# Attention, routed experts and a dense pair of layers on one core: from the routing on, every engine takes its work from one written list

## The chip, the cores and the metric

One core of a Trainium2 chip runs the whole program. It has TensorE (matrix products and, here, all transposes), VectorE, ScalarE, GpSimd and SyncE (SP, which issues most loads). Each engine takes its own instructions in order; between engines they are tied by semaphores. The metric is the device time of one execution in microseconds (us), lower is better.

## The reference

Three steps follow each other on 1536 tokens (2 batches of 768) of width 512 (8 heads of 64).

- Attention: each query sees the keys closer than 16 positions, and beside them 24 summaries, each the maximum of 32 keys (values: the mean), with log 32 added to the score. One softmax over both.
- Routed experts: a token whose product with `w_skip` is not above 0 goes on as it is. Any other token is given to the expert (of 8) with the greatest logit, and becomes `x + gate * (relu(x @ w1[e]) @ w2[e])`, with w1 of 512 x 1024.
- Dense pair: `g(x @ w_in) @ w_out` with 2048 columns between, and `g` 0 below -1, `(h+1)^2/4` up to 1, `h` above. Its weights come as 64-bit floats.

## The kernel before

Attention takes 24 stages of 64 queries by 4 heads' worth of work (`stage_s`, `stage_t`, `stage_pv`: scores, turning of the probabilities, product with the values). When a tile of 128 tokens is complete it is routed: `r1` turns it on TensorE, `r2` multiplies it with the gate (tile `lp`), `r3` takes the maximum and the one-hot on VectorE, `r4` ranks the tokens of an expert by two matmuls with a triangle and with ones (tile `rk`) and works out each token's slot, `r5` scatters the rows by GpSimd to `xf` in device memory. The first 512 rows of `xf` hold tokens that no expert takes; then each expert has a list. `top`, `early` and `late` order the experts by how many tokens they have: position 0 is the largest, known early, positions 1 to 3 are the smallest by what is known after 7 tiles, and positions 4 to 7 the rest. From that order SP reads expert numbers into registers and loads weights.

The first 128 tokens of the largest expert ("first", tiles `fbx`, `hp` of `fb_a`, `yp` of `fb_b`) are gathered early and computed while the last tiles are routed. Then come positions 0 to 7. Each gathers its 32 or 64 rows (one position takes 128 rows more), turns them (`xs`, tile `tpx`), multiplies them by the first layer with the tokens as the stationary side in strips of the array (`as_`, tile `hp`, ScalarE's Relu writes `h`), turns the result (`ts`, tile `tph`), multiplies by the second layer (`bs`, tile `yp`), adds it to the row on VectorE (`ys`) and scatters the row back (`put`). Weights stand in slots of 16 KB a partition named "00" to "13"; a position uses two of them, the first layer and the second, each loaded in two halves (`fetch`, 1.05 MB each). With four pairs of slots position p waits for position p - 4.

The dense pair runs on 3 chunks of 512 tokens. For each of 16 pieces f of the 2048 columns: `mm1` (12 matmuls of 512 columns, tile `hf`), the function `g` on ScalarE and VectorE (`act`), and `mm2` (12 matmuls, tiles `o`). To keep accuracy each operand is split into a rounded half and a rest (`xh`, `xl`, `gh`, `gl`), hence three products. The 64-bit weights are turned into 32-bit ones by three bit operations (`ff_bits`), a rounding on ScalarE and a subtraction on VectorE (`ff_round`), into slots that experts have left. Chunk 0 is the first 512 rows of `xf`, so it needs no expert.

What sets the order: through the attention part every engine follows the order of the code. In the experts' and the dense part only SP and GpSimd do; the order on TensorE, VectorE and ScalarE is drawn from priorities, the place in the code plus the offsets of the table SHIFT. The conversion of the dense weights is a stream of small pieces, of which `fill(n)` places n at a time by the tables FILLS and FFILLS. The four loads of chunk 0's rows stand on SP behind all expert weights (line 857).

Of the kernel before, what the change touches and what calls it, by code (L numbers as in the profile page):

```python
# [42 lines left out]
def tile_net(ctx, tc, q, k, v, w_skip, w_gate, w1, w2, w_in, w_out, out):  # L43
# [12 lines left out]
    xnext = iter(xring * NT)  # L56
# [30 lines left out]
    wg = cp.tile([128, 4, 9], F32, name="wg")  # L87
    placei = cp.tile([1, 18], I32, name="placei")
# [43 lines left out]
    def work_list():  # L132

        def convert(f):
            for step in range(3):
                yield lambda: ff_bits(f, step)
            yield lambda: ff_round(f)

        for f in range(3):
            yield from convert(f)  # L140
            if f:
                for c in (2 * f - 2, 2 * f - 1):
                    yield lambda: st["turn0"](c)
        for f in range(3, NF):
            yield from convert(f)
            if f == YLAST:
                yield lambda: st["ylast"]()

    work = work_list()

    def fill(n):

        for _ in range(n):
            w = next(work, None)
            if w is not None:
                w()

    moves, puts = [], []

    def apart(d, xg, others=()):  # L160

        for o, x in moves:
            if x is not xg and all(x is not y for y in others):
                tc.declare_no_dep(d.ins, o.ins, reason="the blocks have different tokens")
# [13 lines left out]

    @contextmanager
    def shift(name):  # L180
        now = tc.cur_priority
        d = SHIFT.get(name, 0)
        tc.cur_priority = max(0, now + d)
        yield
        tc.cur_priority = now + (tc.cur_priority - max(0, now + d))
# [1110 lines left out]
```

## Time and profile before

| | |
|---|---|
| median of 3 runs | 483.91 us (483.66 to 484.27) |
| the profiled execution | 488.5 us |
| its span, first to last instruction | 486.8 us |
| mean granted clock of TensorE | 0.965 |
| busy: TensorE, VectorE, ScalarE, GpSimd | 455.6, 273.7, 207.9, 70.6 us |
| moved by DMA | 77.19 MB |

A busy TensorE in the profile is one that has a matmul under way, so a busy share near 100% does not say at which clock, or whether the pieces could have come denser; for that the granted clock and the spacing of equal pieces are read. Times in the rows are from the start of the span.

### The profile page before, as it was taken

The numbers are of one execution on the slowest core, as the hardware profiler recorded it, in microseconds if no ns is written. First come the engines' busy times: TensorE is split into PE (matmuls) and PEld (weight loads), VectorE is DVE, ScalarE is ACT, GpSimd is POOL, SyncE is SP. The second block draws the span as 40 slices with busy tenths as digits, with TensorE's granted clock in tenths as the row PEclk, the third lists the DMA queues.
The fourth block names the chain that finished last, engine by engine and source line by source line (L and its number), as shares of the span: only waits on it lengthen the run. The fifth ranks groups of instructions, "written<-read, shape, count | busy, mean of one in ns | idle before, by whom it ended". The sixth has DMA issues, their size and how long they took to land.

```text
span 486.8 us, 8032 instructions
## 1 busy us (share of the span) xinstructions
PE 455.6 (94%) x3010; PEld 332.3 (68%) x3010; DVE 273.7 (56%) x629; ACT 207.9 (43%) x418; POOL 70.6 (15%) x143
## 2 busy tenths in 40 slices
PE   6889999988979995999999999999999999999993
PEld 3567777765434341557778888888888888888882
DVE  3666575785611457599999954433334453333341
ACT  4556555451112122357767765433333443333341
POOL 7001940222330300130000000300000030000003
PEclk9999998995989999699999999999999999999998
DMA  9999999989999999444556600200000020000002
GB/s 196 198 216 194 196 174 230 376 306 374 391 365 398 385 396 380 141 140 140 183 197 224 241 1 25 86 0 1 0 2 0 1 86 0 2 0 1 0 0 94
DMA packets 77104, 77.19 MB, mean 159 GB/s; under 512 B 50606, under 2 KB 58830, under 8 KB 76672
## 3 DMA queue, kind: packets, MB, share of 16 engines
q1 hardware_dynamic: 74176, 68.33, 48.2%
q0 software_dynamic: 2880, 8.25, 4.6%
q8 instruction: 26, 0.43, 0.4%
q14 instruction: 22, 0.18, 0.1%
HBM read 69.44 MB, written 7.76 MB: 159 GB/s over the span
## 4 chain that ended last, share of the span: by engine, by line
issue 42%; PE 29%; DMA 11%; DVE 10%; POOL 5%; SPq 1%; ACT 1%; POOLq 0%; DVEq 0%; ACTq 0%
PE hf L1080 7%; DMA xf<-x,ids 5%; DMA vraw<-in_v_dram 3%; PE s L395 3%; PE o L1121 3%; PE o L1123 2%; PE o L1122 2%; POOL vraw L323 2%; PE hp L229 2%; PE xo L425 2%; POOL out_dram L1133 1%; PE yp L240 1%; PE pt L407 1%; DVE x L914 1%; SPq L303 1%
## 5 line engine op out<-in xcount | busy, mean ns | idle before, releaser
L1080 PE MATMUL hf<-xh,ffw 128*128 128x512 f32 x384 | 126.6, 390 | 0.0
L1080 PEld LDWEIGHTS hf<-xh,ffw 128*128 128x128 f32 x384 | 72.1, 188 | 16.1 <-issue 0.8
L1121 PE MATMUL o<-ffw,g 128*128 128x512 f32 x192 | 76.3, 397 | 0.1
L1122 PE MATMUL o<-ffw,g 128*128 128x512 f32 x192 | 75.5, 393 | 0.0
L1080 PE MATMUL hf<-xl,ffw 128*128 128x512 f32 x192 | 74.9, 390 | 0.0
L1123 PE MATMUL o<-ffw,g 128*128 128x512 f32 x192 | 70.2, 391 | 0.0
L1090 ACT ACTIVATE c<-c,scal 128x512 f32<-128x512 f32 x32 | 23.2, 724 | 74.5 <-DVE c L1089 72.2
L1100 DVE TENSOR_TENSOR hf<-hf,c 128x512 f32<-128x512 f32 x48 | 33.5, 698 | 37.6 <-ACT hf L1098 36.1
L1133 POOL DMA_INDIRECT out_dram<-ob,perm x12 | 11.7, 974 | 247.3 <-DVE ob L1132 162.5
L1106 DVE TENSOR_TENSOR g<-hf,g 128x512 fp32r<-128x512 f32 x48 | 33.1, 690 | 23.4 <-ACT g L1105 23.3
L1089 DVE TENSOR_SCALAR c<-hf 128x512 f32<-128x512 f32 x32 | 22.1, 692 | 40.1 <-PE hf L1080 40.1
L1105 ACT CAST g<-hf 128x512 fp32r<-128x512 f32 x48 | 28.2, 587 | 37.9 <-DVE hf L1100 37.8
L400 ACT ACTIVATE p<-s,nm 128x120 f32<-128x120 f32 x96 | 26.7, 361 | 37.1 <-DVE nm L397 19.8
L1121 PEld LDWEIGHTS o<-ffw,g 128*128 128x128 f32 x192 | 36.1, 188 | 8.8 <-ACT g L1105 1.2
L1123 PEld LDWEIGHTS o<-ffw,g 128*128 128x128 f32 x192 | 36.0, 188 | 8.6 <-DVE g L1106 0.3
L1080 PEld LDWEIGHTS hf<-xl,ffw 128*128 128x128 f32 x192 | 36.1, 188 | 7.5
L1122 PEld LDWEIGHTS o<-ffw,g 128*128 128x128 f32 x192 | 36.1, 188 | 7.0
L914 DVE SCALAR_TENSOR_TENSOR x<-yp,x 32x512 f32<-32x512 f32 (+1 forms) x28 | 20.8, 744 | 10.5 <-PE yp L906 9.6
L395 PE MATMUL s<-pb 64*64 64x120 f32 x384 | 25.7, 275 | 0.0
L397 DVE TENSOR_REDUCE nm<-s 128x4 f32<-128x480 f32 x24 | 15.7, 653 | 15.4 <-PE s L395 12.4
L395 PEld LDWEIGHTS s<-pb 64*64 64x64 f32 x384 | 20.1, 136 | 5.4 <-issue 5.4
L1045 ACT CAST ffw<-cv 128x1024 fp32r<-128x1024 f32 x16 | 16.6, 1046 | 13.3 <-DVE cv L1030 11.4
(221 smaller groups left out, 643.4 us busy)
## 6 DMA issues: line engine op xcount, KB each, us to landing
w<-in_moe_w_dram SPq DMA_DIRECT2D x32, 1024.0 KB, 15.3
raw<-in_moe_w_in_dram SPq DMA_DIRECT2D x16, 512.0 KB, 4.2
raw<-in_moe_w_out_dram SPq DMA_DIRECT2D x16, 512.0 KB
x<-xf SPq DMA_DIRECT2D x12, 264.0 KB, 5.2
raw<-in_k_dram SPq DMA_DIRECT2D x16, 192.0 KB
raw<-in_q_dram SPq DMA_DIRECT2D x16, 192.0 KB, 5.0
vraw<-in_v_dram SPq DMA_DIRECT2D x4, 768.0 KB, 7.8
vw<-in_v_dram SPq DMA_DIRECT2D x13, 192.0 KB, 6.2
```

What stands on the lines that cost most here:

```text
L395: nc.tensor.matmul(s[a, u], tq[a, j], tk[a, j], start=False, stop=u == 3)
L400: nc.scalar.activation(out=p[:, u], in_=s[:, u], func=AF.Exp, bias=nm[:, u:u + 1], scale=1.0)
L914: nc.vector.scalar_tensor_tensor(out=xg[0:n, 0:512], in0=yp[a], scalar=xg[0:n, 512:513], in1=xg[0:n, 0:512], op0=ALU.mult, op1=ALU.add)
L1080: nc.tensor.matmul(hp, w[:, 128 * kk:128 * kk + 128], a[:, kk], start=(n == 0), stop=(n == 11))
L1089: nc.vector.tensor_scalar(out=c, in0=hp, scalar1=-1.0, scalar2=1.0, op0=ALU.max, op1=ALU.min)
L1090: nc.scalar.activation(out=c, in_=c, func=AF.Square, bias=half, scale=0.5)
L1100: nc.vector.tensor_tensor(out=hp, in0=hp, in1=c, op=ALU.add)
L1105: nc.scalar.copy(out=gh, in_=hp)
L1106: nc.vector.tensor_tensor(out=gl, in0=hp, in1=gh.bitcast(F32), op=ALU.subtract)
L1121: nc.tensor.matmul(ops[ch][t], gh[:, a], hi, start=(f == 0), stop=False)
L1122: nc.tensor.matmul(ops[ch][t], gh[:, a], lo, start=False, stop=False)
L1123: nc.tensor.matmul(ops[ch][t], gl[:, a], hi, start=False, stop=(f == NF - 1))
```

## The change

From the end of attention on all engines follow the order of the code. The experts and the first eight pieces of the dense chunk 0 are cut into pieces with one letter each, and one string, ORDER, lists them: X, A, T, B are TensorE's four steps of an expert position, x, a, t, y those of ScalarE and VectorE behind them; U, P, Q, O the same steps of the 128 rows more; R, r, l turn and split chunk 0's rows; M and N are a block of `mm1` and of `mm2`, with c, S, g, G the function between; i, j, k, H, L convert dense weights; F loads a half of a layer of an expert (F40: position 4, half 0), W a piece of dense weights, E gathers rows. After the string, `rest` goes on with piece 8 in fixed steps.

Routing on VectorE is written as generators; `step()` issues one instruction or two of the routing between two instructions of attention, `settle()` the rest. The gather of the block "first" and the loads of position 1 are issued one stage earlier. Position 5 has the 128 rows more (it was 4). Slots: positions 4 and 5 use those of 1 and 2, position 6 those of 3, position 7 those of 5, and the dense weights 0 to 3 those of position 0. The tile of the block "first" stands in another pool (it stood in slot "13"). Chunk 0's 512 rows come in one load into one tile, issued behind the last scatter, with a small one for their token numbers.

```diff
-BIG = (4,)
-ROOM = (64, 32, 32, 32, 160, 32, 64, 32)
+BIG = (5,)
+ROOM = (64, 32, 32, 32, 32, 160, 64, 32)
 LISTS = 1536
 EOFF = 28 * CAP + 8 * LISTS
-SLOTS = (("00", "01"), ("02", "03"), ("10", "11"), ("13", "12"))
-FFSLOTS = ("00", "01", "02", "03", "10", "11", "12", "13")
-NRAW = 4
-FILLS = ((0, 0, 0), (0, 0, 0), (0, 0, 0), (0, 0, 2), (2, 2, 2, 2), (2, 1, 1), (1, 1, 2))
-LAST = 2
-FFILLS = ((2, 1, 2), (2, 0, 2))
-SHIFT = {'bits': 6, 'round': -57, 'act': -1, 'add': -97, 'g': 8, 'y': 18, 'x': -8, 't': 6, 'turn': 0}
-YLAST = 4
-PLACES = {4: 0, 5: 2, 6: 1, 7: 3}
+SLOTS = (("00", "01"), ("02", "03"), ("10", "11"), ("13", "12"), ("02", "03"), ("10", "11"), ("13", "12"), ("10", "11"))
+FFSLOTS = ("00", "01", "02", "03", "13", "12", "10", "11")
+XORDER = (0, 1, 2, 3, 4, 5, 6, 0, 1, 2, 5, 3, 4) + (6, 0, 1, 2, 3, 5, 4, 6, 0) + (1, 2, 3, 4, 5, 6, 0, 1)
+AHEAD = 8
+ORDER = '''
+Z0 i0 j0 k0 X0 x0 A0 X1 a0 x1 T0 H0 A1 t0 L0 B0 F40 a1 i1 F41 j1 k1 W2 H1 R0 y0 F32 R1 F33 r0 R2 r1 l0 r2 l1 R3
+l2 X2 r3 L1 T1 x2 A2 t1 l3 B1 F50 a2 F51 i2 X3 F42 y1 T2 F43 x3 A3 t2 B2 a3 j2 k2 T3 E6 F52 X4 F53 t3 M0 W3 x4
+y2 H2 F60 B3 c0 L2 F61 A4 E7 y3 M1 a4 W4 S0 g0 c1 G0 X5 T4 N0 x5 S1 t4 g1 G1 B4 A5 y4 U0 a5 T5 u0 X6 t5 i3 P0 x6
+j3 k3 W6 H3 B5 F62 F63 p0 L3 P1 y5 A6 p1 i4 j4 k4 W5 H4 Q0 F70 M2 F71 a6 L4 q0 i6 j6 Q1 c2 T6 k6 N1 q1 S2 H6 O0
+t6 L6 g2 G2 i5 j5 k5 H5 M3 F72 o0 F73 L5 W7 B6 c3 S3 X7 y6 g3 M4 x7 G3 A7 c4 i7 M5 j7 a7 S4 k7 g4 N2 c5 G4 i8 j8
+T7 H7 M6 S5 k8 t7 H8 L7 B7 c6 L8 i9 N3 y7 N4 g5 G5 S6 j9 M7 g6 k9 H9 G6 i10 N5 c7 L9 j10 k10 S7 i11 N6 g7 G7 j11
+'''
+PLACES = {4: 2, 5: 0, 6: 1, 7: 3}
...
-            tag = "w" + SLOTS[p % 4][c // 2]
+            tag = "w" + SLOTS[p][c // 2]
...
+        xt, flow = {}, []
+
+        def step():
+
+            while flow:
+                g = flow.pop(0)
+                if next(g, flow) is not flow:
+                    flow.append(g)
+                    return
+
+        def settle():
+            while flow:
+                step()
...
             mx = sm("mx", [128, nt])
             nc.vector.tensor_reduce(out=mx, in_=lt[:, :, 0:8], axis=AX.X, op=ALU.max)
+            yield
             d = sm("d", [128, nt, 8])
             nc.vector.tensor_tensor(out=d, in0=lt[:, :, 0:8], in1=bc(mx), op=ALU.subtract)
             cm = comp[:, ts[0]:ts[0] + nt]
             nc.vector.tensor_scalar(out=cm, in0=lt[:, :, 8], scalar1=0.0, scalar2=None, op0=ALU.is_gt)
+            yield
             val = sm("val", [128, nt, 8])
             nc.vector.scalar_tensor_tensor(out=val, in0=d, scalar=0.0, in1=bce(idx8), op0=ALU.is_lt, op1=ALU.add)
+            nsk = sm("nsk", [128, nt])
...
-            t = wp.tile([128, 12, 128], F32, tag="w13", name="fbx")
-            fb["x"], fb["hT"] = t[:, 0:4], t[:, 4:12]
+            t = b8.tile([128, 16, 128], F32, tag="b8", name="fbx")
+            fb["x"], fb["hT"] = t[:, 0:4], (t[:, 0:4], t[:, 12:16])
+            h = t[:, 4:12].rearrange("p c f -> p (c f)")
...
-        for i in range(3, 2 * NT):
-            if i + 1 < 2 * NT:
-                stage_t(i + 1)
+        for i in range(3, 2 * NT - 1):
+            stage_t(i + 1)
             for _ in range(2 if 5 < i < 8 else 1):
                 if rest:
                     prep(*rest.pop(0))
             if i + 3 < 2 * NT:
                 stage_s(i + 3)
+                step()
             if rest:
                 prep(*rest.pop(0))
-            stage_pv(i)
+            if i == 21:
+                stage_pv(i)
+            for f in pre[i]:
+                f()
+            flow += [f() for f in flows[i]]
+            step()
+            if i != 21:
+                stage_pv(i)
             run_todo(i)
+            step()
+            if i > 15 and i != 18:
+                settle()
+            for f in post.get(i, ()):
+                f()
         for c in range(4):
             fetch(2, c)
-        for f in range(2, NRAW):
-            ff_fetch(f)
-        t, = end = groups[NT - 1]
-        r1(t)
-        r4(of[t - 1])
-        r5(of[t - 1])
+        end, two = groups[NT - 1], groups[NT - 2]
+        fb_x()
+        flow.append(r3(two))
+        step()
+        stage_pv(2 * NT - 1)
+        settle()
+        fb_a(0, (0,))
+        r1(end[0])
+        r4p(two)
+        fb_a(0, (1,))
+        flow.append(r4(two))
+        settle()
         r2(end, 0)
-        fb_x()
-        r3(end)
-        fb_a(0, (0, 1))
-        r4(end)
-        r5(end)
-        late()
         fb_a(0, (2, 3))
-        fb_a(1, range(4))
-        fb_t(0), fb_t(1)
+        flow.append(r3(end))
+        settle()
+        r4p(end)
+        count_p(NT)
+        fb_a(1, (0, 1))
+        fb_a(1, (2, 3))
+        fb_t(0)
+        flow += [r4(end), late()]
+        settle()
+        late_blocks()
+        fetch(3, 0)
+        fetch(3, 1)
+        get_rows()
+        fb_t(1)
         for p in range(NEARLY):
             get(p)
-        fb_b()
+        fb_b(0)
+        fb_b(1)
+        fb_y()
         late_regs()
-        for c in range(4):
-            fetch(3, c)
+        get(4)
         get(BIG[0])
         get((BIG[0], 1))
         st["beyond"] = beyond
 
 
 
-    reads = []
-
...
+    def get_rows():
+
+        t = st["rows"] = b8.tile([128, 4, 512], F32, tag="b8", name="rows")
+        v = xf[0:EARLY].rearrange("(t p) c -> p t c", p=128)
+        for out, c in ((t.bitcast(I32), slice(0, 512)), (perm[:, 0:4].unsqueeze(2), slice(513, 514))):
+            d = nc.sync.dma_start(out=out, in_=v[:, :, c])
+            apart(d, t)
+
+    def get_perm(c, xg):
         nc.vector.tensor_copy(out=perm[:, c:c + 1], in_=xg[:, 513:514].bitcast(I32))
-        return xg
...
+        do = dict(X=X, x=x, A=A, a=a, T=T, t=t, B=B, y=y, U=U, u=u, P=P, p=p_, Q=Q, q=q_, O=O, o=o, Z=Z, R=R, r=r, l=l,
+                  M=M, c=c, S=S, g=g, G=G, N=lambda f: dense.mm2(0, f), H=high, L=low, W=ff_fetch, E=get,
+                  i=lambda f: bits(f, (0,)), j=lambda f: bits(f, (1,)), k=lambda f: bits(f, (2,)),
+                  F=lambda n: fetch(n // 10, n % 10))
+        for word in ORDER.split():
+            do[word[0]](int(word[1:]))
+        dense.rest(AHEAD)
...
+        def step(i, ch, f, n):
             hp = mm1(ch, f)
-
-            act(ch, f, hp, FFILLS[min(i, len(FFILLS) - 1)])
+            c = act(ch, f, hp)
+            runs(n - 1, high)
+            add(hp, c)
+            runs(n, lambda f: bits(f, (2,)))
+            gh(ch, f, hp)
+            gl(ch, f, hp)
+            runs(n - 1, low)
+            runs(n + 1, lambda f: bits(f, (0, 1)))
             if ch + 1 < NC:
...
-        with tc.manual_schedule(engines={EngineType.SP, EngineType.Pool}):
+        with tc.manual_schedule():
             experts(mctx)
-            feed()
     xpool.close()
```

The order on TensorE at the end of the routing, before (`lp` is the last tile's gate product, line 219 the turning of the block "first", `hp_2130` its products, `rk` and `cnt` the last tile's ranks and the counts):

```order
L454 MATMUL lp<-wg,xs 64x9 x8
L219 MATMUL tpx_2108<-ident,x_74 128x128 x4
L229 MATMUL hp_2130<-w_1335,fbx 128x512 x2
L497 LDWEIGHTS tri
L497 MATMUL rk<-ohb,tri 128x8
L498 LDWEIGHTS ones
L498 MATMUL rk<-runs,ones 128x8
L559 LDWEIGHTS ones
L559 MATMUL cnt<-runs,ones 128x8
L229 MATMUL hp_2130<-w_1335,fbx 128x512 x2
```

and of the change, from the first product of the block "first" to the last tile's gate product (`tpx<-ident,x_74` turns the last tile, `rk` are the ranks of the two tiles before it):

```order
L202 MATMUL hp_2057<-w_1336,fbx 128x512
L432 MATMUL tpx<-ident,x_74 128x128 x4
L493 LDWEIGHTS tri
L493 MATMUL rk<-ohb,tri 128x8
L494 LDWEIGHTS ones
L494 MATMUL rk<-runs,ones 128x8
L493 LDWEIGHTS tri
L493 MATMUL rk<-ohb,tri 128x8
L494 LDWEIGHTS ones
L494 MATMUL rk<-runs,ones 128x8
L202 MATMUL hp_2057<-w_1336,fbx 128x512
L443 MATMUL lp<-wg,xs 64x9 x8
```

The turning of "first" and its first product have come ahead of the last tile's turning, and of its first four products, which stood two before and two behind the last tile's ranks, one stands before each matmul step of the routing and two behind `lp`, all ahead of the last ranks.

The order on TensorE from position 2 to 4, before (`yp` second layers, `hp` first layers, `tph` and `tpx` turns; w_2047 and w_2290 are second layers of positions 2 and 3, w_2287 and w_2360 first layers of 3 and 4):

```order
L219 MATMUL tpx<-ident,x_74 128x128 x4
L906 MATMUL yp<-w_2047,hT 32x512 x8
L888 MATMUL hp<-w_2287,xT 32x256 x16
L896 MATMUL tph<-ident,h 128x128 x2
L877 MATMUL tpx<-ident,x_75 128x32 x4
L906 MATMUL yp<-w_2290,hT 32x512 x8
L888 MATMUL hp<-w_2360,xT 32x256 x8
```

and of the change (w_2206 is the first layer of position 3, w_2017 the second of position 2); `hf` is the first dense block:

```order
L1002 MATMUL hp<-w_2206,xT 32x256 x16
L1024 MATMUL yp<-w_2017,hT 32x512 x8
L1012 MATMUL tph<-ident,h 128x128 x2
L990 MATMUL tpx<-ident,x_73 128x32 x4
L1195 MATMUL hf<-xh,ffw 128x512
L1195 MATMUL hf<-xl,ffw 128x512
```

Dense matmuls, which stood behind all experts, now begin behind the second layer of position 2.

SP's queue, before, behind the loads of position 2 (`raw` are dense weights; line 648 reads the late positions' numbers, and position 3's loads follow it):

```order
L1012 DMA raw_2050<-in_moe_w_in_dram 128x4x256
L1014 DMA raw_2050<-in_moe_w_out_dram 128x1024
L1012 DMA raw_2053<-in_moe_w_in_dram 128x4x256
L1014 DMA raw_2053<-in_moe_w_out_dram 128x1024
L648 TENSOR_LOAD placei
```

and of the change, from the second half of position 3's first layer (w_2206) on (`rows` and `perm` are chunk 0's; line 707 reads the late positions' numbers, and position 4's loads follow it):

```order
L136 ISA
L136 DMA w_2206<-in_moe_w_dram 128x2x1024
L961 DMA rows<-xf 128x4x512
L961 DMA perm<-xf 128x4x1
L707 TENSOR_LOAD placei
```

Position 3's first layer and chunk 0's rows stand ahead of the numbers now, and dense weights 2 and 3 behind.

## Rows read from the trace of the kernel before

**Rows 1.** Stretches: length, busy time (x instructions) per engine, granted clock, DMA share, GB/s.
```profile
104.00:136.60 32.60, 26.69 (x152) 14.68 (x147) 20.63 (x128) 6.91 (x17) 11.48 (x12) 0.79 1.02 376
136.60:186.00 49.40, 47.56 (x342) 19.91 (x344) 18.58 (x30) 10.13 (x24) 7.77 (x9) 0.97 1.04 392
186.00:212.30 26.30, 20.58 (x127) 9.00 (x123) 17.80 (x26) 6.81 (x12) 3.94 (x3) 0.81 0.53 190
212.30:252.70 40.40, 40.26 (x176) 32.09 (x173) 38.83 (x46) 29.86 (x45) 3.66 (x2) 1.00 0.55 186
252.70:480.00 227.30, 226.71 (x1010) 186.38 (x1008) 110.08 (x158) 98.29 (x159) 10.20 (x11) 1.00 0.11 40
```

**Rows 2.** Timeline of TensorE, end of routing: start, length, instructions, [idle before, releaser].
```profile
103.43 0.69 PE L425 MATMUL xo<-vw,pts 120*64 120x66 f32 x16
105.71 0.17 PE L497 MATMUL rk<-ohb,tri 128*128 128x8 bf16 x1 [1.59 <-DVE ohb L483]
...
116.38 3.78 PE L229 MATMUL hp<-w,fbx 128*128 128x512 f32 x4 [0.72 <-issue]
119.95 0.21 PE L497 MATMUL rk<-ohb,tri 128*128 128x8 bf16 x1
...
136.64 0.79 PE L877 MATMUL tpx<-ident,x 64*128 64x64 f32 x8 [2.30 <-DMA x<-xf,re]
```

**Rows 3.** The same timeline: an expert's pieces at full rate.
```profile
125.89 0.60 PE L235 MATMUL tph<-ident,fbh 128*128 128x128 f32 x4
...
127.23 7.12 PE L240 MATMUL yp<-w,fbx 128*128 128x512 f32 x16
...
146.22 3.65 PE L906 MATMUL yp<-w,hT 128*64 128x512 f32 x16
149.80 0.44 PE L896 MATMUL tph<-ident,h 128*128 128x128 f32 x2
150.17 1.93 PE L888 MATMUL hp<-w,xT 128*32 128x256 f32 x32
```

**Rows 4.** The same timeline: after the wait for token rows.
```profile
194.96 1.94 PE L219 MATMUL tps<-ident,x 128*128 128x128 f32 x8 [5.52 <-DMA x<-xf]
...
198.08 3.64 PE L906 MATMUL yp<-w,hT 128*32 128x512 f32 x16
```

**Rows 5.** Timeline in the dense part: two blocks' last matmuls, and the last of all.
```profile
457.13 0.39 PE L1080 MATMUL hf<-xh,ffw 128*128 128x512 f32 x1
...
462.60 0.39 PE L1080 MATMUL hf<-xh,ffw 128*128 128x512 f32 x1
...
479.02 0.39 PE L1123 MATMUL o<-ffw,g 128*128 128x512 f32 x1
```

**Rows 6.** Stretch of the dense matmuls alone: those of hf, then of o.
```profile
209.00:252.90 43.90, 24.04 (x96) 18.05 (x97) 9.40 (x14) 13.85 (x23) 1.00 0.51 172
...
209.00:252.90 43.90, 20.45 (x80) 14.71 (x80) 0.00 (x0) 0.00 (x0) 1.00 0.51 172
```

**Rows 7.** Timeline of VectorE, first instruction behind the last rank matmul.
```profile
120.23 0.17 DVE L500 TENSOR_TENSOR sl<-rk,ohb 128x8 f32<-128x8 f32 x1 [3.03 <-PE cnt L559]
```

**Rows 8.** Timeline of GpSimd: first block's gather, last scatter, first expert's gather.
```profile
103.89 1.06 POOL L168 DMA_INDIRECT x<-xf,r  x1 [3.18 <-DVE den L428]
...
122.31 0.97 POOL L173 DMA_INDIRECT xf<-x,si  x1 [4.25 <-DVE nall L563]
129.42 1.23 POOL L168 DMA_INDIRECT x<-xf,re  x1 [6.14 <-DMA xf<-x,si]
```

**Rows 9.** Stretches of 10 us, columns as in rows 1 with GpSimd.
```profile
110.00:120.00 10.00, 8.19 (x52) 4.68 (x50) 5.46 (x38) 1.39 (x4) 2.91 (x3) 0.50 0.99 366
...
150.00:160.00 10.00, 9.42 (x114) 4.27 (x112) 4.06 (x7) 2.62 (x7) 1.90 (x2) 1.00 1.04 397
...
190.00:200.00 10.00, 4.85 (x26) 3.08 (x30) 4.22 (x8) 3.75 (x7) 1.72 (x1) 0.65 0.63 221
```

**Rows 10.** Timeline of SP's queue: loads of expert weights from the fourth expert on.
```profile
134.56 45.65 SPq L129 DMA_DIRECT2D w<-in_moe_w_dram  x20
```

More of the change, by code (lines that the diff above doesn't have):

```diff
@@ L130, in fetch, with apart @@
                           .rearrange("p e k f -> p (e k) f"))
[L132 to L156, printed above, removed]
     moves, puts = [], []
-    def apart(d, xg, others=()):
+    def apart(d, xg):
         for o, x in moves:
-            if x is not xg and all(x is not y for y in others):
+            if x is not xg:
                 tc.declare_no_dep(d.ins, o.ins, reason="the blocks have different tokens")
@@ new lines, in y, with U, u @@
+        def y(p):
+            xg, n, yp = st["x", p], st["n", p], bag.pop(("B", p))
+            for a in sides(n):
+                nc.vector.scalar_tensor_tensor(out=xg[0:n, 0:512], in0=yp[a], scalar=xg[0:n, 512:513],
+                                               in1=xg[0:n, 0:512], op0=ALU.mult, op1=ALU.add)
+            put(p)
+        def U(_):
+            bag["U"] = turned(st["x", more], tile4(128, "tpx"))
+        def u(_):
+            bag["u"] = side("xTm")
+            nc.scalar.copy(out=bag["u"], in_=bag.pop("U"))
@@ new lines, in Q, with q_, O @@
+        def Q(f):
+            tp = bag["Q", f] = tile4(128, "tph")
+            for c in range(4):
+                nc.tensor.transpose(tp[:, c], bag["p"][:, 4 * f + c], ident)
+        def q_(f):
+            if f == 0:
+                bag["q"] = wk.tile([128, 8, 128], F32, tag="hT", name="hTm", bufs=3)
+            nc.scalar.copy(out=bag["q"][:, 4 * f:4 * f + 4], in_=bag.pop(("Q", f)))
+        def O(_):
+            yp = bag["O"] = ps.tile([128, 512], F32, tag="y", name="yp")
+            for kk in range(8):
+                nc.tensor.matmul(yp, bag["q"][:, kk], wx[big, 1][:, kk], start=kk == 0, stop=kk == 7)
@@ new lines, in o, with R, Z @@
+        def o(_):
+            xg = st["x", more]
+            nc.vector.scalar_tensor_tensor(out=xg[:, 0:512], in0=bag.pop("O"), scalar=xg[:, 512:513], in1=xg[:, 0:512],
+                                           op0=ALU.mult, op1=ALU.add)
+            put(more)
+        def R(c):
+            bag["R", c] = turned(st["rows"][:, c], tile4(128, "tps"))
+            if c == 3:
+                st.pop("rows")
+        def Z(_):
+            xTs[0] = tuple(b8.tile([128, 4, 512], F32R, tag="b8", name=n) for n in ("xh", "xl"))
@@ new lines, in r, with l, M, c @@
+        def r(c):
+            nc.scalar.copy(out=xTs[0][0][:, :, 128 * c:128 * c + 128], in_=bag["R", c])
+        def l(c):
+            xh, xl = (z[:, :, 128 * c:128 * c + 128] for z in xTs[0])
+            nc.vector.tensor_tensor(out=xl, in0=bag.pop(("R", c)), in1=xh.bitcast(F32), op=ALU.subtract)
+        dense = feed()
+        def M(f):
+            st["late"] = "h"
+            bag["M", f] = dense.mm1(0, f)
+        def c(f):
+            bag["c", f] = dense.act(0, f, bag["M", f])
+        def S(f):
+            dense.add(bag["M", f], bag.pop(("c", f)))
@@ L1015, in ff_fetch, with bits @@
         raw64[f] = t
[L1017 to L1022 removed]
+    def bits(f, steps=range(3)):
+        for step in steps:
+            if step == 0:
+                odd = f % 2 and f > 6
+                cv[f] = st["wk"].tile([128, 2, 512], I32, tag="h" if odd else "cv", name="cv", bufs=2 if odd else 1)
+            t, o = raw64[f], cv[f]
             if step == 0:
```

468 lines of the change are left out of this document (239 added, 229 removed).

## The prediction

> **What bounds the kernel now.** I read five views, in this order. First the stretches [rows 1]: from 252.7 us TensorE is busy 226.7 of 227.3 us at full clock, from 212.3 to 252.7 it is as full and VectorE is at 38.8 of 40.4 us, so the dense layers are bound by TensorE's matmuls. From 104 to 212.3 us it is not: some 6 us are empty in the first and the third of the three stretches, and the granted clock is 0.79 and 0.81 there. That is where the change works. Then TensorE's rows at the end of the routing [rows 2]: a wait of 1.59 us for VectorE's one-hot, four matmuls at half rate (3.78 us) ahead of the last rank matmul at 119.95, and 2.30 us of waiting for the first gathered tokens, which start to be turned at 136.64. Third, what an expert's pieces cost at full rate [rows 3], and the same piece after TensorE had stood still 5.52 us for token rows [rows 4]: 3.64 us in place of 1.92. Fourth the dense blocks: a pair of blocks, 24 matmuls, repeats every 462.60 - 457.13 = 5.47 us, 0.228 us a matmul, and the last ends at 479.4 [rows 5]. Fifth, how far the dense part is at one moment: by 252.9 us there are 96 + 80 = 176 matmuls done [rows 6], so 180 (eight first-layer blocks M0 to M7, seven second-layer blocks N0 to N6) at 252.9 + 4 x 0.228 = 253.8. From there TensorE needs 479.4 - 253.8 = 225.6 us more.
>
> After the change the same 180 matmuls are the ones that the list holds, among the experts' pieces; what follows is the same 41 + 40 blocks. So the forecast is one number: how much earlier than 253.8 the list's last dense block ends.
>
> **Part by part.** *Routing steps among attention's.* The last rank matmul stands at 119.95. In the new order TensorE has between the end of attention's last-but-two value product (104.1 in [rows 2]) and that matmul: two score matmuls and the last of three (3 x 0.6), the turning of the probabilities, of the last tokens (twice) and of the first block (4 x 0.6), two value products (2 x 0.7), four of the first block's matmuls (a run of eight takes 7.12 [rows 3], so 4 x 0.9) and the ranks (0.6): 9.8 us, plus about 0.7 us of copies between them: 114.6. The wait of 1.59 goes, since the one-hot's steps are issued one stage earlier, and so does the half-rate surplus (3.78 x 1/2) if the clock holds. The first block is turned before the last value product now: its gather, issued at 103.89 [rows 8], must have landed by 108. Its row numbers are worked out one stage (2.9 us) earlier, so I count no wait; its cost, if it landed as late as the later gather's 7.2 us after today's issue, is 3 us. VectorE reaches its first routing instruction behind the rank at 120.23 today after idling 3.03 us for it [rows 7], and the last scatter is issued at 122.31, 2.1 us on; now some 20 instructions of two chains stand there instead of 12, which I take as 0.7 us more. The scatter then goes out at 114.6 + 0.3 + 2.8 = 117.7, 4.6 us earlier [rows 8]. From it to the first turned tokens are 136.64 - 122.31 = 14.3 us, a scatter's landing and a gather's, and both remain.
>
> *The load of the first 512 rows* (1.05 MB) now waits on SP for the same scatter and so moves with the gather; at 397 GB/s [rows 9] that is 2.6 us of all queues. Bounds for the gather: 0, when the queues share and its few bytes come first, and 2.6 + 5.3 us when it stands behind that load and the two loads of the fourth expert (2 x 1.05 MB) that SP now issues before it. I take 1 us, near the lower end, since the gather of today landed in 7.2 us while [rows 1] show 376 GB/s of other traffic, so it did not wait for a queue to drain. The Trainium skill, page DMA: Bandwidth & Descriptors, section Queues, rings and completion order, says that a DMA engine takes turns between the queues that have work, a packet at a time; by it the sum would be as here, by first come first served it would be the second rival below; no row here shows two queues' turns apart. First turned tokens: 136.6 - 4.6 + 1 = 133.0, a gain of 3.6.
>
> *The list.* From there to the 180th matmul takes 253.8 - 136.6 = 117.2 us today. TensorE's own work in that stretch, at full rate: 15 dense blocks x 2.735 = 41.0; first layers of the experts, two of 64 rows at 3.65 and six of 32 at 1.93, 18.9; second layers the same again, 18.9; the extra 128 rows of the large expert, twice 7.12 as the first block's, 14.2; and the turns, 14 small ones at 0.44 and nine at 0.6, 11.6 [rows 3, 5]. Sum 104.6, and the surplus of today is 12.6: 5.5 idle [rows 4], the rest half-rate stretches (0.65 in 190 to 200 [rows 9], worth 3.5 us) and small waits. In the list the rows wait goes, since the 512 rows are turned right after the first expert, some 60 us before the other experts end. What is late next: copies that nothing covers (first tokens' copy 0.7, first activations 0.4, the four row turns behind three PSUM buffers 1.3, some eight of 0.2 to 0.5 later), 4 us; the wait before the first tokens, which grows: the first block ends at 114.6 + 13 = 128, so TensorE stands still some 5 us instead of 2.30, and by the stall of 5.52 us, behind which the pieces are at half rate until 201.7, 6.7 us on [rows 4], I take 8 us at half rate, which cost 4. Bounds for this surplus of mine: 3 (only copies) to 16 (each piece also waits once for its weights). I take 8, so the list gives 12.6 - 8 = 4.6.
>
> *Weights.* A half of an expert's layer is 1.05 MB, 2.6 us at 397 GB/s [rows 9]. The places changed: expert 5 waits for expert 2's, expert 8 for expert 6's. The fifth expert's loads stand on SP behind the second expert's first layer (133.0 + 8 = 141), where SP today starts 20 loads at 134.56 [rows 10]; queues run dry for up to 10 us before it. From 141 on, 22 loads come at 2.6 us in the list's order; the second layer of the fifth expert lands at 167 and is wanted at 171, the seventh's first layer 181 against 186, the last expert's first layer 200 against 214. Its second layer waits for the large expert (203), lands at 211, and is wanted at 225; the dense chunk behind it on SP lands at 213, when VectorE reaches it. So I cost waiting for weights at nothing, with slack of 4 to 14 us; where SP, waiting at its head, is 5 us later than this, the cover is gone.
>
> *Strict order in the dense part.* Today the last matmuls of a block are drawn behind three of the next; now a block's third matmul needs its lower half at once. VectorE needs 38.83/40.4 of its time today [rows 1]; per pair of blocks the new order has the same six instructions. Between 0 and +3 us for the six pairs with conversions left; I take 0.
>
> **Sum.** 3.6 + 4.6 = 8.2 us off the profiled execution, 488.5 (span 486.8) to 480.3. The runs without the profiler have a median of 483.91, 4.6 below; the same difference gives 475.7.
>
> **Rivals.** *All waits covered, clock kept*: the surplus is 3 and the gather costs nothing: 4.6 + 9.6 = 14.2 us, 469.7. For it: only 104.6 us of work in 117; against it: the empty stretch before the first tokens.
> *Gathers behind the loads*: the first tokens come 7.9 us after my 132.0, at 139.9; the list then leaves 4.6 - 3.3 = 1.3: 482.6. Half of that delay gives 478.7. For it: scatter and gather took 14.3 us with the queues full; against it: 7.2 us was enough for the gather.
> *Slower, through the clock*: the place is TensorE from the first tokens on. After 1.6 us of waiting at 104 us the granted clock was 0.50 for 110 to 120 [rows 2, 9], and a stall of 5.5 us brought 0.65. Every microsecond at half rate costs 0.5. If the wait of 5 us and the copies' gaps keep the clock at 1.2 GHz for 16 us beyond my 8, the 8.2 are gone; for 25 us the result is 483.9 - 8.2 + 12.5 = 488.2. It decides from 16 us on. The Trainium skill, page TensorE: Matmul & The Clock Gate, section HAM oscillation — how this bites in real kernels, tells of matmuls that start slow after each wait for a DMA; by that rule every such wait of the list would be paid twice, and the trace agrees at 194.96. Against it: M and N blocks, dense and long, stand between the experts from the fourth on, and in the dense part of today the clock is 1.00 throughout [rows 1].
> *The list is not followed in time*: engines wait for each other as long as before, within 1 us of today, 484.
>
> **Chances.** Forecast 0.55 (471 to 479), all covered 0.13, gathers late 0.17, no change 0.04, slower 0.11. The range 467 to 482 takes in the first three but leaves out the far ends. A change of 0.2%, 1 us, is about what this kernel's runs can tell. Faster 0.85, same 0.04, slower 0.11.
>
> **What would show it.** Last rank matmul near 115 and last scatter near 118; first tokens turned at 132 to 134; the 5.5 us wait for rows gone; granted clock above 0.9 from 140 to 235; the 180th dense matmul near 245.6; no wait of TensorE for a weight over 1 us; 225 to 226 us from there to the last matmul. I am wrong if the first tokens stay near 136.6, if the clock stays at half past 150, or if TensorE waits for weights.

## The result, and the profile after

The changed kernel takes 477.32 us, the median of 4 runs (476.84 to 477.85), beside 484.09 us (483.66 to 484.82) for the kernel before: ratio 0.9859, with a 95% interval of 0.9842 to 0.9876. Measured again beside other runs later, the ratio was 0.9837 (0.9807 to 0.9868). It is faster by 1.4 to 1.6%, some 7 to 8 us. The forecast was 475.7, in a range of 467.0 to 482.0. Its profiled execution took 477.85 us.

First the stretches of [rows 1], here of the changed kernel (columns as there).

```profile
104.00:136.60 32.60, 24.76 (x131) 12.42 (x127) 14.16 (x98) 4.56 (x11) 10.72 (x11) 0.86 0.99 373
136.60:186.00 49.40, 47.64 (x378) 23.82 (x376) 34.10 (x46) 19.77 (x39) 9.86 (x9) 0.99 0.91 336
186.00:212.30 26.30, 26.27 (x109) 14.85 (x106) 19.91 (x25) 11.98 (x19) 3.28 (x3) 1.00 1.00 364
212.30:252.70 40.40, 39.39 (x204) 29.97 (x203) 31.46 (x38) 23.54 (x37) 1.33 (x2) 1.00 0.47 162
252.70:480.00 227.30, 214.40 (x952) 175.18 (x951) 99.72 (x146) 90.24 (x145) 11.69 (x12) 0.99 0.09 34
```

The third line is where the time came from: TensorE busy 26.27 of 26.30 us at full clock, where it was 20.58 at 0.81. VectorE is at 34.10 of 49.40 us in the second line (19.91 before) and at 31.46 of 40.40 in the fourth (38.83 before): its conversions now lie beside the experts. In the first line TensorE is busy for less time than before (24.76 against 26.69 us), at a higher mean clock (0.86 against 0.79): about as much of the stretch is still lost to waiting and half rate.

TensorE's timeline at the end of the routing shows where; it answers to [rows 2].

```profile
104.59 0.64 PE L443 MATMUL lp<-wg,xs 128*64 128x9 f32 x16 [0.16 <-ACT xs L433]
108.79 1.11 PE L192 MATMUL tpx<-ident,x 128*128 128x128 f32 x4 [3.56 <-DMA x<-xf,r]
...
110.92 2.08 PE L202 MATMUL hp<-w,fbx 128*128 128x512 f32 x2
...
117.13 0.17 PE L493 MATMUL rk<-ohb,tri 128*128 128x8 bf16 x1
...
132.60 0.43 PE L990 MATMUL tpx<-ident,x 64*128 64x64 f32 x4 [2.87 <-DMA x<-xf,re]
133.61 5.35 PE L1002 MATMUL hp<-w,xT 128*64 128x512 f32 x16 [0.58 <-ACT xT L994]
```

The waits for one-hots near the end are gone, but TensorE now stands 3.56 us for the first block's gathered tokens, and the last value product, the last tokens and the last ranks stand behind that wait in its order. Behind it the matmuls run at half rate, 2.08 us for two; and behind the second wait, 2.87 us for the first expert's tokens, its first layer takes 5.35 us where it takes 3.65 at full rate. GpSimd's timeline, which answers to [rows 8]:

```profile
101.34 1.06 POOL L149 DMA_INDIRECT x<-xf,r  x1 [6.32 <-PE pt L381]
...
119.53 0.97 POOL L154 DMA_INDIRECT xf<-x,si  x1 [1.70 <-DVE ve L186]
126.47 1.09 POOL L149 DMA_INDIRECT x<-xf,re  x1 [5.97 <-DMA xf<-x,si]
```

The first gather is issued at 101.34, only 2.5 us earlier than before, while TensorE wants it some 9 us earlier: at 105.2, against 114.55 in the kernel before, whose row is

```profile
114.55 1.12 PE L219 MATMUL tpx<-ident,x 128*128 128x128 f32 x4
```

The last two lines of GpSimd's timeline put the end of the routing at 119.53 and the first expert's gather at 126.47; its tokens are turned at 132.60, 6.1 us later.

In the dense part, the end of the list (the last matmul of N6, and M8's first), the two waits of TensorE behind it and the start of the last matmul:

```profile
240.45 0.39 PE L1238 MATMUL o<-ffw,g 128*128 128x512 f32 x1
240.68 0.39 PE L1195 MATMUL hf<-xh,ffw 128*128 128x512 f32 x1
...
272.41 0.66 PE L1177 MATMUL tpf<-ident,x 128*128 128x128 f32 x4 [1.04 <-DVE xl L1185]
...
464.21 0.50 PE L1236 MATMUL o<-ffw,g 128*128 128x512 f32 x1 [0.75 <-ACT g L1219]
...
468.50 0.40 PE L1238 MATMUL o<-ffw,g 128*128 128x512 f32 x1
```

So the path divides like this: first turned tokens 136.64 to 132.60, 4.0 us gained; from there to the end of the list 117.2 to 108.1 us, 9.1 gained; from the end of the list to the start of the last matmul 225.2 us (479.02 - 253.8, [rows 5, 6]) to 227.8, 2.6 lost. That is 10.5 us between these two profiled executions, more than the 6.8 us between the medians: the profiled execution of the kernel before lay above its runs (488.5 beside 484.1).

### The profile page after: what moved, and what is told of

Its sections match the earlier page's. It is cut to its first block, busy times and chain, and to the rows that moved or that the text cites. A ratio compares the mean times of both kernels' runs of the same rounds, so it can differ in the third digit from the quotient of the medians.

```text
span 476.1 us, 8008 instructions
## 1 busy us (share of the span) xinstructions
PE 446.3 (94%) x3010; PEld 327.1 (69%) x3010; DVE 266.1 (56%) x625; ACT 208.8 (44%) x418; POOL 70.0 (15%) x143
## 4 chain that ended last, share of the span: by engine, by line
PE 38%; issue 37%; DMA 8%; DVE 6%; SPq 5%; ACT 2%; POOL 2%; POOLq 0%; DVEq 0%; ACTq 0%
PE hf L1195 6%; PE s L369 4%; SPq L277 3%; PE hp L1002 3%; DMA raw<-in_moe_w_out_dram 3%; PE o L1236 3%; PE o L1237 3%; PE o L1238 2%; PE xo L411 2%; PE yp L1024 2%; PE pt L381 2%; DVE x L1029 2%; DMA vw<-in_v_dram 2%; POOL out_dram L1248 2%; DMA x<-xf,r 2%
## 5 line engine op out<-in xcount | busy, mean ns | idle before, releaser
L1236 PE MATMUL o<-ffw,g 128*128 128x512 f32 x192 | 76.3, 398 | 0.7 <-ACT g L1219 0.7
L1237 PE MATMUL o<-ffw,g 128*128 128x512 f32 x192 | 75.5, 393 | 0.0
L1238 PE MATMUL o<-ffw,g 128*128 128x512 f32 x192 | 75.0, 391 | 0.0
L1204 ACT ACTIVATE hf<-hf,scal 128x512 f32<-128x512 f32 x32 | 21.2, 662 | 85.1 <-DVE c L1203 85.1
L1157 DVE TENSOR_TENSOR ffw<-cv,ffw 128x1024 fp32r<-128x1024 f32 x16 | 19.5, 1219 | 12.8 <-ACT ffw L1152 12.8
```

What stands on the lines that cost most here:

```text
L1204: nc.scalar.activation(out=hp, in_=hp, func=AF.Relu, bias=mone, scale=1.0)
L1236: nc.tensor.matmul(ops[ch][t], gh[:, a], hi, start=(f == 0), stop=False)
L1237: nc.tensor.matmul(ops[ch][t], gh[:, a], lo, start=False, stop=False)
L1238: nc.tensor.matmul(ops[ch][t], gl[:, a], hi, start=False, stop=(f == NF - 1))
```

## The experiments

All times are medians; each ratio is to the kernel before, run on the same chip in the same session. That kernel took 484.1, 487.4, 488.0, 484.9 and 484.6 us in the five sessions, so ratios are compared, not microseconds. The four later sessions ran on different chips; what is the session's and what is the chip's is not told apart here. The control e0 ran beside e5, e7 and e11; e1, e2, e4 and e6 share a session, e8, e9 and e12 another, and e14 has its own.

| run | us | ratio, 95% interval |
|---|---|---|
| changed kernel, first measurement | 477.3 | 0.9859 (0.9842 to 0.9876) |
| e0_control, the same again | 479.6 | 0.9837 (0.9807 to 0.9868) |
| e2_dense_behind | 514.1 | 1.0560 (1.0515 to 1.0605) |
| e5_experts_first | 505.4 | 1.0354 (1.0328 to 1.0381) |
| e9_rows_late | 499.5 | 1.0299 (1.0276 to 1.0323) |
| e6_no_interleave | 480.1 | 0.9845 (0.9810 to 0.9880) |
| e4_value_first | 480.8 | 0.9862 (0.9833 to 0.9891) |
| e11_value_then_first | 480.3 | 0.9855 (0.9822 to 0.9888) |
| e7_turn_first | 477.7 | 0.9785 (0.9756 to 0.9813) |
| e8_busy_before_tokens | 474.1 | 0.9792 (0.9758 to 0.9826) |
| e12_busy_twice | 472.5 | 0.9738 (0.9717 to 0.9758) |
| e14_value_first_busy | 473.4 | 0.9773 (0.9748 to 0.9799) |

**e0_control** was expected at a ratio of 0.984 to 0.988, with a wait of 0.5 to 3.6 us for the first block's gather and 105 to 110 us from the first turned tokens to the 180th dense matmul. The ratio was 0.9837, the wait 4.02 us, both just outside, and the stretch 108.3 us:

```profile
134.10 0.43 PE L990 MATMUL tpx<-ident,x 64*128 64x64 f32 x4 [2.76 <-DMA x<-xf,re]
...
242.43 0.39 PE L1195 MATMUL hf<-xh,ffw 128*128 128x512 f32 x1
...
470.25 0.40 PE L1238 MATMUL o<-ffw,g 128*128 128x512 f32 x1
```

**e1_before_again**: the kernel before, a second profile.

> The kernel before, unchanged, for a second profile. Theory A: the 4.6 us by which its profiled execution (488.5) lies above the runs without a profiler (484.1) belong to that one execution, in the stretch between the first turned tokens (136.64) and the 180th dense matmul (253.8), 117.2 us there: the second profile shows about 484 and 112 to 114 us in that stretch, with the first tokens near 136.6 again. Rival B: the profiler always costs this kernel 4.6 us: the second profile shows 488 and 117 us again.

It took 486.6 us in a session whose median was 487.4. TensorE's timeline of this second profile of the kernel before:

```profile
134.16 0.43 PE L877 MATMUL tpx<-ident,x 64*128 64x64 f32 x4 [1.11 <-DVE ids L207]
...
194.13 1.94 PE L219 MATMUL tps<-ident,x 128*128 128x128 f32 x8 [8.24 <-DMA x<-xf]
...
251.75 1.09 PE L1123 MATMUL o<-ffw,g 128*128 128x512 f32 x4
...
477.45 0.39 PE L1123 MATMUL o<-ffw,g 128*128 128x512 f32 x1
```

Neither theory holds. The profiled execution is not above the runs beside it, so the profiler costs nothing that shows. The 4.6 us are then most likely a difference between executions or sessions; in which session the first profile was taken, the record doesn't say. And the stretch to the 180th dense matmul is long again: 180 have begun by 252.2, 118.0 us behind the first tokens. Two more things are to be seen. The first tokens come at 134.16, 2.5 us before those of [rows 2], with the same code: where the routing ends differs by that much from one execution to the next. And TensorE gained little by it: it waits 8.24 us instead of 5.52 for the token rows, which come at 194.13 against 194.96. In the kernel before, most of what came earlier at the routing's end was given back at the rows: 0.8 of the 2.5 us is left there. Set against e0, this profile divides the gain otherwise than the first pair: 0.1 us at the first tokens (134.16 to 134.10), 9.7 in the list (118.0 to 108.3), 2.6 lost behind it (225.2 to 227.8). That is 7.2 us, near the 6.8 of the runs, and nearly all of it is the list's.

**e2_dense_behind and e5_experts_first**: the dense layers' pieces taken out from among the experts.

```
 e2: ORDER = (all pieces but M c S g G N, in their order) + (M c S g G N, in their order)
 e5: as e2, and i j k H L of chunks 4 and up, W6, W7 also moved behind the last expert
```

> The changed kernel with the 47 pieces of the dense layers' arithmetic (M, c, S, g, G, N) moved in the list behind the last expert, in their own order; the conversions and the loads stay where they are. Theory A: the dense blocks among the experts cover the loads of expert weights. From 140 us some 18 half layers and 6 dense chunks of 1.05 MB have to land, 24 x 2.6 = 63 us, so the last expert cannot be done before about 205; the 15 dense blocks, 41 us, then stand behind it, and the 180th dense matmul comes near 250 in place of 240.7: about 487 us (483 to 491), with waits of TensorE for weights that sum to about 10 us. Rival B: what the list gives comes from the early token rows and the clock that is kept, and the place of the dense blocks is indifferent: 476.5 to 478.5 us.

> The changed kernel with its list sorted: the experts' pieces first, with the early turning of the 512 rows, the conversions of the dense chunks 0 to 3 and the loads of chunks up to 5 where they stand; behind the last expert all arithmetic of the dense layers and the conversions from chunk 4 on, in their own order. Theory A: among the experts the dense blocks cover loads. 22 loads of 1.05 MB from about 140 us on take 57 us, so the last expert's second layer cannot start before 197 to 200, and M0 to N6 with their conversions take 44 us behind that, as they did before (209.6 to 253.8): the 180th dense matmul at 244 to 247 and 4 to 7 us more than the unaltered changed kernel, with TensorE's waits for weights before 200. Rival B: the early rows are the whole gain, experts and dense part could as well stand apart: within 1 us of the unaltered one, with the 180th dense matmul near 241.

Both cost far more than theory A said, in the direction that it said. The waits of TensorE of 140 to 270 us, first e2, then e5:

```profile
PE yp L1024 <- ACT hT L1016: 12.0, 1, 12.0
PE o L1236 <- ACT g L1219: 10.3, 1, 10.3
PE yp L1024 <- DMA w<-in_moe_w_dram: 5.3, 3, 4.2
```

```profile
PE hf L1195 <- ACT ffw L1152: 9.3, 1, 9.3
PE yp L1024 <- DMA w<-in_moe_w_dram: 5.6, 4, 4.1
```

Weights are waited for directly (5.3 and 5.6 us), in e2 half of the 10 us expected. The long waits are of another kind. In e2 ScalarE's copy for the last expert stands in the list behind the rounding of a chunk whose load lands at 213.6, and so TensorE stands 12.0 us for an expert whose weights SP had issued at 199.04, ahead of that chunk. An engine that follows a list passes one late load on to everything behind it. In e5 the conversions came too late instead: VectorE is at 6.61 of 26.30 us from 186 to 212.3 and the chunk is then missing at 244.9. So without the dense blocks among the experts this list loses more than its whole gain; how much of the 26 to 35 us is loads, and how much these two lists' own faults, the runs don't separate. Nor does a run give the kernel before the early load of the 512 rows alone, so whether that needed the written order stays open.

**e9_rows_late**: the one load of 512 rows put behind weights on SP.

```
-        get_rows()                    # ahead of the expert loads
+ ORDER: ... F42 y1 T2 F43 Y0 ... F53 t3 R0 r0 R1 l0 r1 R2 l1 r2 R3 l2 r3 l3 M0 ...   (Y0 = get_rows)
```

> The unaltered changed kernel but for the load of the first 512 rows, which stands on SP behind the loads of the second layer of the fifth expert and not ahead of all of them, and their turning and splitting right before the first dense block M0. Theory A: a load that SP issues behind the weights lands behind them, as the rows did before: SP paces these loads at 2.6 us each from 144.6 on, so the rows are issued near 158 and land 5 to 13 us later; TensorE waits at M0 (158) for 6 to 14 us, and half rate follows: 8 to 16 us over the unaltered changed kernel, 488 to 496 us, ratio 1.000 to 1.017. Rival B: the queues share, a row load is served beside the weights: a wait of at most 3 us, 480 to 484 us, ratio under 0.993.

Theory A holds, and more: SP's issue of the rows, TensorE's wait, and the load's time from issue to landing.

```profile
155.75 4.34 SPq L960 DMA_DIRECT2D rows<-xf  x1
```

```profile
173.39 1.94 PE L192 MATMUL tps<-ident,rows 128*128 128x128 f32 x8 [18.77 <-DMA rows<-xf]
```

```profile
DMA to landing us min/median/max: 17.5/17.5/17.5
```

A load of 1.05 MB that SP issues behind eight half layers and a dense chunk lands 17.5 us later, and TensorE waits 18.77 us where at most 14 were expected; the kernel takes some 22 us more than the control (0.0462 of 485). The gather that GpSimd issued among the same traffic, at 159.48, landed in 6.3 us (381 GB/s from 155 to 172). Both agree with what the Trainium skill, page DMA: Bandwidth & Descriptors, section Queues, rings and completion order, states: a DMA engine takes turns between queues, but consumes one queue's descriptors in order.

**e6_no_interleave**: each routing chain run to its end at once.

```
                 if next(g, flow) is not flow:
                     flow.append(g)
-                    return
```

> The changed kernel with each routing chain run to its end where its next step would stand, instead of one step at a time among attention's instructions. Theory A: single steps hide the latency of a chain; run in one piece, the normalising of attention's values waits behind them on VectorE and TensorE's waits for one-hots come back, as before (1.59 and 0.73 us): the first tokens come about 2 us later, 479.5 us (478.5 to 481). Rival B: VectorE has room enough, the order of its steps is worth nothing: 476.6 to 478 us.

Rival B has the better of it: 0.9845 (0.9810 to 0.9880) against 0.9837 of e0, another session. The waits for one-hots did not come back; TensorE waits 2.08 us at 97.87 instead, and the first tokens come at 133.76, within the spread of the other profiles. Weaving single routing steps among attention's is worth nothing that can be measured here; the interval leaves room for 1.7 us either way.

**e4_value_first and e11_value_then_first**: attention's last value product ahead of the first block.

```
-        fb_x()
         flow.append(r3(two)); step(); stage_pv(2 * NT - 1); settle()
-        fb_a(0, (0,))
         r1(end[0])
+        fb_x(); fb_a(0, (0,))         # e11; in e4 both stand behind r4p(two) and r2(end, 0)
```

> The changed kernel with the turning of the first block's tokens moved behind attention's last value product, the last tokens' turn and the last logits; all of the first block's first-layer matmuls but one stand behind the last rank matmul. Theory A: TensorE's 3.56 us of waiting for the first block's gather holds back the routing's end behind it; now the wait stands behind what the last ranks need, so the last rank matmul comes at 111 to 113 (117.1 in the changed kernel), the last scatter at 114 to 116 (119.5), the first tokens are turned at 128 to 130 (132.6), when the first block ends: about 474 us (472.5 to 475.5). Rival B: from the last scatter to the first turned tokens the queues full of weights decide, or the weights do later: first tokens stay near 132.6, or a wait for weights takes their gain, 476.5 to 478 us.

> The changed kernel with attention's last value product and the last tokens' turn ahead of the first block's turned tokens; otherwise the order of the routing's end is kept, with the first block's matmuls between the steps of the rank chain. Theory A: the wait for the first block's gather holds back only what stands behind it; taken out of the rank chain, the last rank matmul comes 2.5 to 3.5 us earlier (113.5 to 115), the last scatter with it, the first tokens are turned at 129 to 130.5, and the time is 2.5 us (1.5 to 3.5) under the unaltered changed kernel. Rival B: the end of the first block on TensorE takes the scatter's place, as when all of it stood behind the ranks: first tokens at 131 to 132.5, less than 1 us.

Theory A fails in both times. In e4 the last rank matmul comes at 115.05 and the last scatter at 117.23, earlier than in the changed kernel though not as early as expected; but the first block, begun later and at half rate, then ends on TensorE at 131.4, and the first tokens are turned at 132.24. In e11 the last rank matmul (118.36) comes 12.3 us behind the last logits but one, 12.5 in the changed kernel, and the first tokens at 133.65: taking the wait out of the chain gained nothing there. Why, no run shows.

**e7_turn_first**: the next chunk's tokens ahead of a conversion on VectorE.

```
             gl(ch, f, hp)
+            (turn, get_perm, parts of the next chunk)
             runs(n - 1, low)
             runs(n + 1, lambda f: bits(f, (0, 1)))
-            (turn, get_perm, parts of the next chunk)
```

> The changed kernel with, in the loop of the dense part, the turning and splitting of the next chunk's tokens moved ahead of the lower half of a weight chunk and the next chunk's bits on VectorE. Theory A: TensorE's wait of 1.04 us at 272.41 (1.2 us with the restart) is a queue on VectorE, where a split of tokens stands behind a conversion of 1.2 us that is not wanted yet: the wait goes and nothing takes its place: 1.2 us less than the unaltered changed kernel (0.6 to 1.6). Rival B: VectorE is busy for 19.14 of 20 us there and only changes what is late: a wait of the same size for a lower half, 0 us.

Theory A holds: 0.9785 against 0.9837, in the same session, and no run of either kernel lies among those of the other. The medians differ by 1.9 us, more than the 0.6 to 1.6 expected; the trace accounts for 1.1. The wait at 272 is gone, and from the end of the list to the last matmul's start it is 226.7 us in place of 227.8. Nearly half of what the strict order cost was one conversion of 1.22 us that stood ahead of a split wanted sooner.

**e8_busy_before_tokens and e12_busy_twice**: TensorE kept busy in its two waits (on top of e7).

```
+        def idle_work(n): o = ps.tile(...); n x nc.tensor.matmul(o, tri, masks[0], ...)
...
+        idle_work(20)                 # e12 only
         fb_x()
...
         fb_y()
+        idle_work(26)                 # e8, e12
```

> The kernel with the turn moved ahead on VectorE, and 26 matmuls of 240 columns on constants, some 2.6 us, put in TensorE's order between the first block's last matmul and the first turned tokens, where TensorE waits 2.7 to 2.9 us; nothing reads their result. Theory A: the half rate behind a wait is paid in full: the first expert's first layer takes 3.65 us in place of 5.35, so the 180th dense matmul comes 1.7 us earlier behind the first tokens (106.5 us after them in place of 108.2) and the time is 1.5 us (0.8 to 2) under that of the kernel without these matmuls, ratio to the kernel before near 0.9755. Rival B: the pieces behind wait for copies and weights anyway, and what the first layer gains is lost within the next 20 us: 0 us, ratio 0.9785.

> As the run with matmuls on constants before the first turned tokens, and 20 more of them (2 us) before the first block's turn, where TensorE waits 0.6 to 4 us for that block's gather. Theory A: half rate behind that wait stretches the first block's matmuls that stand between the steps of the rank chain (2.08 in place of 1.1 us each) and with them the last rank matmul; at full rate the last scatter comes 1.5 to 2 us earlier and the first tokens too: 1.5 us (0.5 to 2.5) under the run with one such stretch. Rival B: the chain from the last value product to the last scatter is VectorE's and the copies', and the matmuls on constants delay it where the gather has landed early: 0 to 1 us more.

In e12, TensorE's timeline at the end of the routing:

```profile
106.98 2.22 PE L819 MATMUL idle<-mask,tri 128*128 128x240 bf16 x20
110.53 0.66 PE L192 MATMUL tpx<-ident,x 128*128 128x128 f32 x4 [1.33 <-DMA x<-xf,r]
111.12 0.69 PE L411 MATMUL xo<-vw,pts 120*64 120x66 f32 x16
111.91 1.13 PE L202 MATMUL hp<-w,fbx 128*128 128x512 f32 x2
...
116.92 0.17 PE L493 MATMUL rk<-ohb,tri 128*128 128x8 bf16 x1
...
129.36 2.83 PE L819 MATMUL idle<-mask,tri 128*128 128x240 bf16 x26
132.34 0.43 PE L997 MATMUL tpx<-ident,x 64*128 64x64 f32 x4
133.35 3.65 PE L1009 MATMUL hp<-w,xT 128*64 128x512 f32 x16 [0.58 <-ACT xT L1001]
```

Work that nobody reads keeps the clock: two of the first block's matmuls take 1.13 us in place of 2.08, the expert's first layer 3.65 in place of 5.35. The granted clock of 104 to 114 us, in the changed kernel and then in e12:

```profile
104.00:114.00 10.00, 6.28 (x63) 4.41 (x58) 2.86 (x20) 1.27 (x4) 1.98 (x2) 0.66 1.03 378
```

```profile
104.00:114.00 10.00, 8.26 (x105) 6.41 (x104) 4.64 (x38) 2.39 (x6) 1.98 (x2) 1.00 1.02 385
```

From the turn of the first block to the last rank matmul it is 6.4 us, against 8.3 in the changed kernel, and the median falls by 1.65 us against e8 in the same session, as theory A has it; the intervals of the two ratios just touch. The two profiled executions took the same time (474.1 and 474.2 us), since in that of e12 attention ended 3.2 us later; counted from the last logits but one, its last scatter goes out at 13.1 us in place of 14.9 and its first tokens are turned at 26.1 in place of 28.3. For the stretch before the first tokens the evidence is weaker: in e8's profile the list takes 106.75 us (238.10 - 131.35) in place of 108.2, but its ratio, 0.9792, is not below that of e7. That one stays open.

**e14_value_first_busy**: e4's order with the clock kept.

> The order of the run with the value product first (the first block's turn behind the last logits), with the turn of the next chunk's tokens moved ahead on VectorE, and 20 matmuls of 240 columns on constants (2.2 us) behind the last value product, where TensorE waits 1.96 us for the values; none before the first turned tokens. Theory A: the value product first gained nothing because the first block's matmuls then ran at half rate (10 us in place of 7.1) and ended at 131.4; at full rate the last scatter goes out 10.2 us behind the last logits but one (11.3 there, 13.1 in the run with two stretches of matmuls on constants) and the first block ends in time: first tokens 23.5 us behind those logits in place of 26.1, ratio to the kernel before 0.966 to 0.971. Rival B: the path from the scatter to the gathered tokens, or the first block on TensorE, gives back what the ranks gain: ratio 0.973 to 0.979.

The profile shows what theory A expects, the times do not. TensorE, then GpSimd's last scatter:

```profile
104.19 0.64 PE L443 MATMUL lp<-wg,xs 128*64 128x9 f32 x16 [0.16 <-ACT xs L433]
...
111.97 0.17 PE L493 MATMUL rk<-ohb,tri 128*128 128x8 bf16 x1
...
127.45 0.46 PE L995 MATMUL tpx<-ident,x 64*128 64x64 f32 x4 [0.84 <-DVE x L750]
```

```profile
114.11 0.97 POOL L154 DMA_INDIRECT xf<-x,si  x1 [1.70 <-DVE ve L186]
```

The last scatter goes out 9.9 us and the first tokens come 23.3 us behind the last logits but one (13.1 and 26.1 in e12), and this execution took 470.87 us. But the five runs lie between 470.87 and 475.16, and the ratio is 0.9773. The profiled one is the fastest of them; what the others lose, no trace shows. The best median ratio of the study is that of e12: 0.9738, some 1% under the changed kernel; the intervals of e12 and e14 overlap.

## Why the prediction was right, and where it was not

The direction, the size and the main mechanism, a list that keeps TensorE supplied, were right; the terms were not. That 8.2 us forecast came so near to 6.8 measured is in part luck: their errors cancelled.

- **Routing, 4.6 us at the last scatter and 3.6 at the first tokens: too much.** The first pair of profiles has 2.8 and 4.0, and e1 with e0 has none, 0.1 us at the first tokens. Six profiles in which the routing's code is that of the changed kernel (its own, e0, e2, e5, e7, e9) put the first tokens at 130.83 to 134.56, mean 132.9, and two of before come at 136.64 and 134.16: about 2.5 us, and uncertain by as much. The failing step is "so I count no wait" for the first gather, bounded there at 3 us. The wait was 0.6 to 4.0 us in the six: TensorE came for the tokens 9 us earlier and the gather was issued only 2.5 us earlier. It goes out 4.8 to 8.1 us behind the scatter ahead of it; that it waits for this scatter to land is likely, but no row names it. And the wait put the half rate on the last ranks, which the text let go "if the clock holds". It did not: 0.66 from 104 to 114 (1.00 in e2, where the wait was 0.6 us).
- **The load of the first 512 rows, 1 us: nothing.** From the issue of the first expert's gather to its turned tokens it is 6.1 us with that load beside it, 7.2 and 6.25 in the two profiles of the kernel before, and 6.2 in e9, the same kernel with the load elsewhere.
- **The list, 4.6 us: 9.1.** The mis-sized term is the surplus over TensorE's own 104.6 us: I took 8, between 3 and 16; it is 3.5 (108.1, 108.3 and 108.2 in three profiles). The wait for the first tokens is 2.9 us, not 5, since the first block ends later than I had it (129.7, not 128); and behind it only the first layer is slow, which costs 1.7 us and not 4. No piece waits for weights, as forecast; without the dense blocks among the experts TensorE does wait for them (e2, e5), and that the rows are early is needed too (e9).
- **Strict order, 0 within 0 to 3 us: 2.6.** Two waits, 1.04 us at 272.41 and 0.75 us at 464.21, each costing its idle time and a slower restart. e7 takes the first away.
- **From the trace to the runs, 4.6 us: nothing.** The forecast in the trace was 480.3, and the changed kernel's profiled execution took 477.85. The step that failed is "the same difference gives 475.7": a profiled execution need not lie above the runs (e1), and that of the changed kernel did not.
- **Rivals.** "All waits covered" was the nearest to the list's real surplus; "gathers behind the loads" is out for GpSimd's gathers and right for SP's own loads (e9). "Slower, through the clock" had a cost that is there, but small: half rate takes 1.7 us behind the first tokens, where it looked for it, and some 2 us at the routing's end (8.3 against 6.4), where it did not. The rule of the Trainium skill, page TensorE: Matmul & The Clock Gate, section HAM oscillation — how this bites in real kernels, that matmuls behind a wait for data start slow, agrees with 2.08 against 1.13 us.

## What to carry to other kernels

When one engine's order is written out as a list, the long independent matmuls belong between the pieces that wait for loads, and every load's place on its queue counts, because a late one holds up all that stands behind its first user. A move that makes an engine arrive earlier gains nothing where the data's own chain sets the time; look first at what issues the gather, not at who waits for it. And before a trace is compared with runs, profile the same kernel twice: here two pairs of profiles divided the same gain in two ways.

## What was not expected of the hardware

Matmuls on constants for 2.2 and 2.8 us, put into waits of some 3 us, were enough in e12 to keep TensorE's granted clock at 1.00 from 104 to 136.6 us. In e9 a load on SP's queue took 17.5 us from issue to landing while a gather of GpSimd's took 6.3 us among the same 381 GB/s. And one kernel took 484.1 to 488.0 us from session to session, 0.8%, the four later ones on different chips, with the start of its experts 2.5 us apart in two profiles.
